# The two heads' first scores in one slot: shifting dense products by two scores in a fused attention and MLP kernel

## The chip, the cores and the metric

The kernel runs on one core of one Trainium2 chip. The metric is the device time of one execution in microseconds (us). The kernel before takes 1265.47 us (median of 3 runs, 1265.09 to 1265.52).

## The reference

One input of 2048 tokens by 512 channels goes through two branches that are mixed by a gate for each token:

```python
H = 32; Dh = D // H                                   # S = 2048, D = 512, F = 1792
q, k, v = (x @ wqkv) split into 32 heads of 16
p = softmax((q @ k^T) * Dh**-0.5)                     # 32 x 2048 x 2048
a = (p @ v, heads joined) @ wo
h = layernorm(x)
u = gelu(einsum("bsd,sf->bdf", h, w1) + b1)           # over tokens
b = einsum("bdf,fs->bds", u, w2) + b2, transposed
g = sigmoid((x * gate_w).sum(-1))
out = g * a + (1 - g) * b
```

All of it is in float32. Where the kernel uses single-pass float32 products, it splits an operand in a high and a low part and adds three products.

## The kernel before, in words

**Stages.** Up to about 278 us the kernel makes v, k, half of q and the first layer of the MLP. All that follows but the last few microseconds is one long loop of 128 *phases* (line 994), and the change is in this loop. Dense work that is left (the second MLP layer, the other half of q, the first half of the output projection) is done inside the loop, beside the attention scores.

**A phase.** Two heads and half of the queries (1024) make a *group*; 32 groups of four phases each. A phase makes 16 *scores*: score n is one product of 128 keys by 512 queries of one head, transposed (keys on partitions), 64 rows deep (16 channels in three split products and a shift). Head 0's operands lie on partitions 0 to 63 and head 1's on 64 to 127, so a score uses half of TensorE's rows. The other half can at the same time do a *dense product* (line 1076), half of the rows of a 128-row product; the other 64 rows are done in the next phase. Even phases (`second` = 0) have their scores on head 0 and dense halves on rows 64 to 127, odd phases (`second` = 1) the other way round. Two matmuls that run side by side are called a *slot* here. A phase has `n_b` = 14 dense products (96 phases) or 12 (32 phases): in phases 0 to 63, the last two of every eight have 12 (a late query block), phases 64 to 111 all have 14, and phases 112 to 127 all have 12 (the output projection). A score that has no dense product beside it is paired with a score of the other head, which `head` says. A group's first phase is called ph 0.

**What becomes of a score.** It lies in PSUM, in one of seven banks, and goes one of three ways:

```python
EVAC = 1, 3, 5, 9, 14, 15        # VectorE copies it to SBUF (L1089); one long exp over all six (L1102)
SINGLE = 0, 2, 4, 6, 7, 8        # ScalarE's exp reads it from PSUM (L1093)
TWO = (10, 11), (12, 13)         # ScalarE's exp reads two neighbouring banks at once (L1031)
TURNS = [(0, 2), (4, 6), (7, 8), *TWO]
HELD = [(1, 3), (5, 9), (14, 15)]
```

ScalarE (ACT) does in each phase six single exps in order of n, two double ones, and the long exp; nothing else in most of the loop. The profile names the scores' tiles s (scores 0 to 9), t (10 to 13) and u (14 and 15).

**Banks.** Scores 0 to 6 take the seven banks. Score 7 takes that of score 0 (freed by the first single exp), 8 that of score 1 (first copy), 9 that of score 2 (second single). Scores 10 and 11 take those of 3 and 4 (second copy, third single), 12 and 13 those of 5 and 6 (third copy, fourth single), 14 that of 7 (fifth single), 15 that of 9 (fourth copy). The result of p @ v, `av`, takes that of score 8 (sixth single).

**The end of a phase.** `apply_v` (line 953) multiplies the exps with v in 64 matmuls of 128 rows by 32 columns, four side by side: first the pairs HELD of the phase before, then the pairs TURNS of this one. VectorE (DVE) then adds `av` to the group's sums (L985). In ph 0 the held pairs are the last of the group before and go to a bank of their own, so there are adds for `av` and adds for a second bank (`t`). Which part of the bank an add covers follows from the heads of the pairs: if all pairs have one head, one add of 128x256; two adds, 128x256 and 64x256, if one pair has both heads; one add of 128x512 if all is met.

**Order.** The loop is under `manual_schedule`, so every engine executes in the order in which the program is written. The copies of the next phase stand behind the adds of this one in DVE's queue. A token that GpSimd (POOL) writes after a phase's last dense product (L1080) keeps the first dense product of the next phase behind it, since both add to the same bank `dn`. When the last product of a dense block is done, DVE reads `dn`: at the end of the phase in most cases, but in the eight second phases of a late query block a copy `begin` (L616) is put ahead of the copies of scores 14 and 15 (line 1084), at the score before the last.

Of the kernel before, what the change touches and what calls it, by code (L numbers as in the profile page):

```python
# [60 lines left out]
def gated_mix(ctx: ExitStack, tc: tile.TileContext, a_x, a_wqkv, a_wo, b_w1, b_b1, b_w2, b_b2, gate_w, out):  # L61
# [55 lines left out]
    def bank():  # L117
        return acc.tile([P, NB], F32, name="acc")
# [59 lines left out]
    with tc.tile_pool(name="vp", bufs=1, side="right") as pool:  # L178
# [122 lines left out]
        for t in range(2, NS):  # L301
# [9 lines left out]
            ps = bank()  # L311
# [51 lines left out]
    if True:  # L363

        def project(w, n):
            ps = bank()
            cols = slice(n * NB, (n + 1) * NB)
            hi, lo = w
            products(ps, [((hi[:, k, :], lo[:, k, :]), (xt_hi[:, k, cols], xt_lo[:, k, cols])) for k in range(ND)])
            return ps  # L370
# [12 lines left out]
        for b in range(ND):  # L383
            wk_b, wq_b = qk_w.pop(0), qk_w.pop(0)
            kmax = bd.tile([P, NQ], F32, name="kmax")
            for at, (n, keys) in enumerate(jobs):
                ps = project(wk_b if keys else wq_b, n)
# [38 lines left out]
    with tc.tile_pool(name="gl", bufs=2, side="right") as gl:  # L426
# [22 lines left out]
        beside = {mybir.EngineType.Activation, mybir.EngineType.DVE, mybir.EngineType.Pool}  # L449
# [51 lines left out]
        for f0, cs in order.items():  # L501
            n = min(NB, F - f0) // P
            ps = [bank() for _ in range(n)]
# [77 lines left out]
    PHASES, NSC, BANKS = 4, 16, 7  # L581
# [295 lines left out]
    for t in range(NS):  # L877
        at = put(second_layer(t), at, [14] * 3)
        if queries:
            b, n = queries.pop(0)  # L880
# [53 lines left out]
    def regions():  # L934
        return tc.tile_pool(name="ps_s", bufs=1, space=PSUM, reuse_waits="tile")
# [3 lines left out]
    def column_halves(x):  # L939
        x = x.rearrange("p (i m c) -> p m i c", i=2, m=2)  # L940
        return x[:, 0], x[:, 1]
# [48 lines left out]
    with tc.manual_schedule(engines=engines):  # L990
        held, fence, turn, spare = [], None, 0, 0
        landed.clear()

        for p in range(LAST + 1):
            grp, ph = divmod(p, PHASES)
            second = ph % 2
# [10 lines left out]
            if not second:  # L1007
                beside = [step(*args) for step, *args in dense.get(p // 2, ())]
            n_b = len(beside)
            half = slice(0, HALF) if second else slice(HALF, P)  # L1010

            head = [second if n < n_b else (second + NSC - 1 - n) % 2 for n in range(NSC)]
            if n_b == NSC - 2:
                head[-2:] = second, 1 - second
            else:
                head[-4:] = second, 1 - second, 1 - second, second
            in_turn = list(range(n_b)) + ([14, 15] if n_b == NSC - 2 else [12, 13, 15, 14])
            qbs = {}
            for a, b in TURNS + HELD:
                if head[a] == head[b]:  # L1020
# [6 lines left out]
            def exps(n):  # L1027
                pt = ptp.tile([P, 2, NB], F32, name="p2", bufs=len(TWO))
                where = [share[(j - BANKS) % BANKS] for j in (n - 1, n)]
                low = min(where)  # L1030
                pairs_done.append(nc.scalar.activation(pt, twos[low, low + 1], AF.Exp, scale=SCALE))  # L1031
                for j, k in zip((n - 1, n), where):
                    units[j] = *units[j][:3], pt[:, k - low, :]
# [8 lines left out]
            for n in in_turn:  # L1042
                i, qb = head[n], qbs[n]
                c = at[i][qb]
                at[i][qb] += 1
                if n < TWO[0][0]:
                    if n >= BANKS:
                        ones[share[n - BANKS]] = psum.tile([P, NB], F32, name=f"s{share[n - BANKS]}")
                    s = ones[share[n % BANKS]]
                else:  # L1050
                    if n == TWO[0][0]:
                        pool.__exit__(None, None, None)
                        pool = regions()
                        psum = pool.__enter__()
                        twos = {}
                        for low in range(BANKS):
                            if low == share[1]:
                                av = psum.tile([P, NB], F32, name="av")
                            elif low in (share[0], share[2]):
                                twos[low] = psum.tile([P, NB], F32, name=f"u{low}")  # L1060
                            elif low not in twos:
                                two = psum.tile([P, 2, NB], F32, name=f"t{low}")
                                twos[low], twos[low + 1] = two[:, 0, :], two[:, 1, :]
                                twos[low, low + 1] = two
                    s = twos[share[2 if n == NSC - 1 else (n - BANKS) % BANKS]]
                rows_i = slice(i * HALF, i * HALF + ROWS)
                nc.tensor.matmul(  # L1067
                    s,
                    kt[grp][rows_i, c * P : (c + 1) * P],
                    qt[grp][rows_i, qb * NB : (qb + 1) * NB],  # L1070
                    start=True,
                    stop=True,
                )
                if n < n_b:
                    ps, a, b, begin, last, done = beside[n]
                    mm = nc.tensor.matmul(ps, a[half], b[half], start=begin and not second, stop=last and bool(second))  # L1076
                    if n == 0 and fence is not None:
                        tc.add_manual_dep(mm.ins, fence.ins.name, SYNC, reason=REASON)
                    if n == n_b - 1:
                        fence = nc.gpsimd.memset(token, 0.0)  # L1080
                        tc.add_manual_dep(fence.ins, mm.ins.name, SYNC, reason=REASON)
                if n == in_turn[-2]:
                    if n_b and second and beside[-1][-1] in between:
                        between[beside[-1][-1]]()
                    for what, *args in amid.get(p, ()):
                        what(*args)
                if n in EVAC:
                    pt = evac[:, EVAC.index(n), :]
                    nc.vector.tensor_copy(pt, s)  # L1089
                    units[n] = i, c, qb, pt  # L1090
                elif n in SINGLE:
                    pt = ptp.tile([P, NB], F32, name="p1", bufs=len(SINGLE))
                    one = nc.scalar.activation(pt, s, AF.Exp, scale=SCALE)  # L1093
                    if n == SINGLE[-1] and p:
                        tc.add_manual_dep(one.ins, earlier.ins.name, SYNC, reason=EARLY)
                    units[n] = i, c, qb, pt
                else:
                    units[n] = i, c, qb, None
                    if n in (TWO[0][1], TWO[1][1]):
                        exps(n)  # L1100
            for x in ([evac] if p < LAST else [evac[:, :2, :], evac[:, 2:, :]]):
                done = nc.scalar.activation(x, x, AF.Exp, scale=SCALE)  # L1102
# [45 lines left out]
    with (  # L1148
# [17 lines left out]
        last = column_halves(last_ot)  # L1166
# [63 lines left out]
    with tc.If(far_off != 0):  # L1230
        with (
# [6 lines left out]
            for b in range(ND):  # L1238
                with tc.For_i(0, P // DH, 1) as hi:
# [11 lines left out]
                    for t in range(NS):  # L1251
# [4 lines left out]
                        m = pool.tile([P, 1], F32, name="m")  # L1256
# [54 lines left out]
```

## Time and profile before

| | |
|---|---|
| median of the runs | 1265.47 us (1265.09 to 1265.52) |
| profiled execution | 1265.31 us, of which the span of its instructions 1263.5 us |
| granted TensorE clock | 0.999 |
| loop of phases | first single exp at 278.1 us, the last exp ends at 1229.5 us (1226.48 + 2.97) |

How to read the rows: a group of instructions is given with its line, engine, operation, out<-in tiles and shape, its count, the engine's busy time, the mean duration in ns, and the idle time before it with what ended it. In a timeline a row has start, duration (of the whole run of like instructions that are merged to one row, xcount), engine, line and operation, and in brackets the idle time before it. PE are matmuls, PEld their weight loads. Durations of neighbouring instructions of one engine overlap, so the step from start to start is shorter than the duration. Matmul ends are modelled.

### The profile page before, as it was taken

The numbers are of one execution on the slowest core, as the hardware profiler recorded it, in microseconds if no ns is written. First come the engines' busy times: TensorE is split into PE (matmuls) and PEld (weight loads), VectorE is DVE, ScalarE is ACT, GpSimd is POOL, SyncE is SP. The second block draws the span as 40 slices with busy tenths as digits, with TensorE's granted clock in tenths as the row PEclk, the third lists the DMA queues.
The fourth block names the chain that finished last, engine by engine and source line by source line (L and its number), as shares of the span: only waits on it lengthen the run. The fifth ranks groups of instructions, "written<-read, shape, count | busy, mean of one in ns | idle before, by whom it ended". The sixth has DMA issues, their size and how long they took to land.

```text
span 1263.5 us, 32833 instructions
## 1 busy us (share of the span) xinstructions
PE 1254.8 (99%) x13342; PEld 829.2 (66%) x13342; DVE 856.7 (68%) x1562; ACT 1069.0 (85%) x1405; POOL 198.6 (16%) x316
## 2 busy tenths in 40 slices
PE   9999999999999999999999999999999999999998
PEld 7888888875666666666666666666666666666656
DVE  5675453178767676767677677776777677678883
ACT  4443343269999999999999999999999999999990
POOL 0220444461010101010110101111111111000000
PEclk9999999999999999999999999999999999999999
DMA  4799443244744444544344433444543443366611
GB/s 134 251 340 329 143 122 106 81 127 110 214 121 104 90 102 85 158 86 97 77 105 94 99 90 83 91 87 81 113 101 73 90 100 60 56 166 175 151 60 70
DMA packets 100556, 152.32 MB, mean 121 GB/s; under 512 B 17109, under 2 KB 56171, under 8 KB 96300
## 3 DMA queue, kind: packets, MB, share of 16 engines
q1 hardware_dynamic: 99820, 149.08, 46.0%
q8 instruction: 107, 1.75, 0.6%
q10 hardware_dynamic: 576, 1.05, 0.2%
q14 instruction: 53, 0.43, 0.1%
HBM read 105.39 MB, written 44.68 MB: 119 GB/s over the span
## 4 chain that ended last, share of the span: by engine, by line
PE 96%; DVE 2%; ACT 1%; issue 0%; DVEq 0%
PE av L963 31%; PE s L1067 21%; PE acc L424 12%; PE t L1067 9%; PE acc L75 8%; PE t L963 5%; PE dn L1076 3%; PE u L1067 3%; PE pa L1162 2%; DVE pe L1089 1%; PE acc L199 1%; PE acc L268 0%; DVE ot L985 0%; PE acc L245 0%; ACT p L1093 0%; ACT pe L1102 0%
## 5 line engine op out<-in xcount | busy, mean ns | idle before, releaser
L1093 ACT ACTIVATE p<-s 128x512 f32<-128x512 f32 x768 | 411.9, 789 | 0.1
L1102 ACT ACTIVATE pe<-pe 128x3072 f32<-128x3072 f32 x129 | 380.9, 2954 | 0.0
L1067 PE MATMUL s<-qs,ks 64*128 64x512 f32 x1280 | 329.8, 400 | 0.6 <-ACT p L1093 0.6
L1089 DVE COPY pe<-s 128x512 f32<-128x512 f32 x512 | 323.6, 685 | 5.5 <-PE s L1067 1.5
L1067 PEld LDWEIGHTS s<-qs,ks 64*128 64x128 f32 x1280 | 225.7, 184 | 92.7 <-issue 52.3
L1031 ACT ACTIVATE p<-t 128x1024 f32<-128x1024 f32 x256 | 278.7, 1267 | 0.0
L963 PE MATMUL av<-p,v 128*32 128x256 f32 x3880 | 227.2, 379 | 0.0
L1089 DVE COPY pe<-u 128x512 f32<-128x512 f32 x256 | 164.8, 685 | 67.1 <-PE u L1067 67.1
L963 PE MATMUL av<-pe,v 128*32 128x256 f32 x3072 | 192.5, 383 | 0.0
L985 DVE TENSOR_TENSOR ot<-av,ot 128x512 f32<-128x512 f32 (+2 forms) x160 | 93.0, 582 | 140.9 <-PE av L963 139.6
L68 POOL TENSOR_TENSOR w_lo<-w_raw,w_hi 128x512 fp32r<-128x512 f32 (+1 forms) x128 | 153.0, 1202 | 196.8 <-ACT w_hi L67 99.9
L1076 PE MATMUL dn<-u_lo,w_hi 64*128 64x512 f32 x448 | 181.0, 404 | 0.0
L1076 PE MATMUL dn<-u_hi,w_hi 64*128 64x512 f32 x448 | 180.7, 403 | 0.0
L963 PEld LDWEIGHTS av<-p,v 128*32 128x32 f32 x3880 | 126.0, 110 | 83.3 <-ACT p L1093 0.2
L1076 PE MATMUL dn<-u_hi,w_lo 64*128 64x512 f32 x448 | 180.6, 403 | 0.0
L1067 PE MATMUL t<-qs,ks 64*128 64x512 f32 x512 | 142.5, 413 | 0.0
L963 PEld LDWEIGHTS av<-pe,v 128*32 128x32 f32 x3072 | 86.8, 109 | 80.7 <-ACT p L1093 35.7
L1080 POOL MEMSET token<- 1x1 f32 x128 | 11.3, 88 | 742.7 <-PE dn L1076 679.4
L67 ACT CAST w_hi<-w_raw 128x512 fp32r<-128x512 f32 (+1 forms) x67 | 38.0, 569 | 82.7 <-PE acc L424 63.1
L1067 PEld LDWEIGHTS t<-qs,ks 64*128 64x128 f32 x512 | 73.2, 184 | 50.8 <-ACT p L1093 48.6
L424 PE MATMUL acc<-h_hi,w_hi 128*128 128x512 f32 x224 | 87.9, 392 | 0.0
L424 PE MATMUL acc<-h_hi,w_lo 128*128 128x512 f32 x224 | 87.9, 392 | 0.0
(171 smaller groups left out, 1615.8 us busy)
## 6 DMA issues: line engine op xcount, KB each, us to landing
w_raw<-in_B_w_dram SPq DMA_DIRECT2D x96, 256.0 KB
ks<-kp SPq DMA_DIRECT2D x192, 128.0 KB
qs<-qp SPq DMA_DIRECT2D x256, 64.0 KB
kp<-pc SPq DMA_DIRECT2D x16, 512.0 KB
qp<-pc SPq DMA_DIRECT2D x8, 768.0 KB
qp<-row SPq DMA_DIRECT2D x24, 256.0 KB
v<-v SPq DMA_DIRECT2D x4, 1088.0 KB
x<-in_A_x_dram SPq DMA_DIRECT2D x16, 256.0 KB
```

Source lines behind the costliest of these rows:

```text
L67: copy(hi, src)
L68: return sub(lo, src, hi.bitcast(F32), ALU.subtract)
L75: nc.tensor.matmul(ps, a, b, start=start and n == 0, stop=stop and n == last)
L424: nc.tensor.matmul(p, a, b, start=first and k == 0, stop=last and k == 2)
L963: mm = nc.tensor.matmul(av[32 * j : 32 * (j + 1), i * QC : (i + 1) * QC], vb[b][:, v_at : v_at + 32], pt[:, h * QC : (h + 1) * QC], start= ...
L985: latest["add"] = nc.vector.tensor_tensor(x, y, x, ALU.add)
L1031: pairs_done.append(nc.scalar.activation(pt, twos[low, low + 1], AF.Exp, scale=SCALE))
L1067: nc.tensor.matmul(s, kt[grp][rows_i, c * P : (c + 1) * P], qt[grp][rows_i, qb * NB : (qb + 1) * NB], start=True, stop=True,)
L1076: mm = nc.tensor.matmul(ps, a[half], b[half], start=begin and not second, stop=last and bool(second))
L1089: nc.vector.tensor_copy(pt, s)
L1093: one = nc.scalar.activation(pt, s, AF.Exp, scale=SCALE)
L1102: done = nc.scalar.activation(x, x, AF.Exp, scale=SCALE)
```

## The change

The order in which a phase's scores are paired is changed. Before, score n stood beside dense product n from the first slot on, and the scores that were left over stood at the end: 14 and 15 as a pair of the two heads (`n_b` = 14), or 12 and 13 and then 15 and 14 (`n_b` = 12). After, scores 0 and 1 are a pair of the two heads in the first slot, dense product m stands beside score m + 2, and where there are 12 dense products scores 14 and 15 are a second pair of the two heads at the end. The scores are issued in plain order.

With it, other scores belong to the other head: score 1, and with 12 dense products score 15 too, where it was score 15 (14 dense products) or 13 and 14 (12). So with 12 dense products all pairs in TURNS now have one head; the pair (1, 3) in HELD has both.

```diff
-            head = [second if n < n_b else (second + NSC - 1 - n) % 2 for n in range(NSC)]
-            if n_b == NSC - 2:
-                head[-2:] = second, 1 - second
-            else:
-                head[-4:] = second, 1 - second, 1 - second, second
-            in_turn = list(range(n_b)) + ([14, 15] if n_b == NSC - 2 else [12, 13, 15, 14])
+            head = [second] * NSC
+            head[1] = 1 - second
+            if n_b < NSC - 2:
+                head[-1] = 1 - second
+            in_turn = range(NSC)
...
-                if n < n_b:
-                    ps, a, b, begin, last, done = beside[n]
+                m = n - 2
+                if 0 <= m < n_b:
+                    ps, a, b, begin, last, done = beside[m]
                     mm = nc.tensor.matmul(ps, a[half], b[half], start=begin and not second, stop=last and bool(second))
-                    if n == 0 and fence is not None:
+                    if m == 0 and fence is not None:
                         tc.add_manual_dep(mm.ins, fence.ins.name, SYNC, reason=REASON)
-                    if n == n_b - 1:
+                    if m == n_b - 1:
                         fence = nc.gpsimd.memset(token, 0.0)
                         tc.add_manual_dep(fence.ins, mm.ins.name, SYNC, reason=REASON)
```

## The prediction

> **What bounds the kernel now.** I read the page's busy line and costliest groups first, then the timeline of ScalarE (ACT), then that of PE and VectorE (DVE) in one phase.
>
> ```profile
> PE 1254.8 (99%) x13342; PEld 829.2 (66%) x13342; DVE 856.7 (68%) x1562; ACT 1069.0 (85%) x1405; POOL 198.6 (16%) x316
> ...
> L1093 ACT ACTIVATE p<-s 128x512 f32<-128x512 f32 x768 | 411.9, 789 | 0.1
> L1102 ACT ACTIVATE pe<-pe 128x3072 f32<-128x3072 f32 x129 | 380.9, 2954 | 0.0
> ...
> L1089 DVE COPY pe<-s 128x512 f32<-128x512 f32 x512 | 323.6, 685 | 5.5 <-PE s L1067 1.5
> ```
>
> PE looks full, but a matmul's end is modelled. The exps are what counts: no idle time stands before them (0.1 and 0.0 us).
>
> ```profile
> 709.36 3.24 ACT L1093 ACTIVATE p<-s 128x512 f32<-128x512 f32 x6
> 712.23 2.19 ACT L1031 ACTIVATE p<-t 128x1024 f32<-128x1024 f32 x2
> 714.08 3.00 ACT L1102 ACTIVATE pe<-pe 128x3072 f32<-128x3072 f32 x1
> 716.77 3.24 ACT L1093 ACTIVATE p<-s 128x512 f32<-128x512 f32 x6
> ```
>
> One phase on ACT: six single exps, two double ones, one exp over the six copied scores; 716.77 - 709.36 = 7.41 us, and 128 phases of it are most of the span. Is ACT the limit, or is it fed at just that pace? A disturbed stretch tells:
>
> ```profile
> 857.72 3.25 ACT L1093 ACTIVATE p<-s 128x512 f32<-128x512 f32 x6
> 860.60 2.21 ACT L1031 ACTIVATE p<-t 128x1024 f32<-128x1024 f32 x2
> 862.73 2.77 ACT L1102 ACTIVATE pe<-pe 128x3072 f32<-128x3072 f32 x1
> 865.40 3.02 ACT L1093 ACTIVATE p<-s 128x512 f32<-128x512 f32 x6
> ...
> 872.73 3.12 ACT L1093 ACTIVATE p<-s 128x512 f32<-128x512 f32 x6
> ...
> 880.05 3.21 ACT L1093 ACTIVATE p<-s 128x512 f32<-128x512 f32 x6
> ```
>
> Here the long exp began 862.73 - 860.60 = 2.13 us after the double ones, against 714.08 - 712.23 = 1.85: 0.28 late. Afterwards the six singles start every 7.33 and 7.32 us, but they end at 868.42, 875.85 and 883.26: every 7.43 and 7.41. So ends come at 7.41 to 7.43 a phase whatever the starts do. Of the 0.28 lost at 862.73, only 880.05 - 857.72 - 3 x 7.41 = 0.10 was left three phases later. I read this as ACT's own pace, 7.42, with a lead: in the quiet phase instructions are begun about 3.24 - 3.02 = 0.22 us before their turn. That lead is the cover under which PE or DVE may be late at no cost.
>
> Now who feeds it:
>
> ```profile
> 708.82 0.50 PE L1067 MATMUL s<-qs,ks 64*128 64x512 f32 x1
> ...
> 712.01 0.39 PE L1067 MATMUL t<-qs,ks 64*128 64x512 f32 x1
> 712.01 0.38 PE L1076 MATMUL dn<-u_hi,w_hi 64*128 64x512 f32 x1
> 712.24 0.43 PE L1067 MATMUL u<-qs,ks 64*128 64x512 f32 x2
> 712.65 1.50 PE L963 MATMUL av<-pe,v 128*32 128x256 f32 x24
> 713.97 2.34 PE L963 MATMUL av<-p,v 128*32 128x256 f32 x40
> 716.24 0.50 PE L1067 MATMUL s<-qs,ks 64*128 64x512 f32 x1
> ```
>
> A loop is seen: score 0 at 708.82, its exp 0.53 later (716.24 to 716.77), the sixth single ends at 709.36 + 3.24 = 712.60, which frees the bank of av; av starts at 712.65, and the next score 0 follows 716.24 - 712.65 = 3.59 later. 0.53 + 3.24 + 0.05 + 3.59 = 7.41: closed. With ACT without its lead (3.02) it would be 7.19, so the PE side has 0.22 to spare, and no more.
>
> **The change part by part.** The instructions are the same in number and shape: 16 scores, 14 (96 phases) or 12 (32 phases) dense products, 9 exps, 6 copies, 64 av matmuls a phase, and the DMAs and their order stay. A slot, two matmuls side by side, costs 712.24 - 712.01 = 0.23, and there are 15 or 14 before and after. What moves:
>
> (1) *Start of a phase.* Score 1 takes the place of the first dense product in the cold slot; scores 2 to 14 come one slot earlier. Nothing is gained by it: exps go in ACT's order, and the banks of scores 7 to 13 come free at the pace of exps and copies. Zero for the slot itself. The first dense product waits for POOL's token of the phase before, which now comes one slot later, but some 3.5 us of av hide that. SP and POOL are passed by nothing else.
>
> (2) *End of a phase with 14.* Today scores 14 and 15 share a slot at 712.24; now each stands beside a dense product, one slot more behind the second pair of scores. Two rows tell when av may start:
>
> ```profile
> 1120.50 0.50 PE L1067 MATMUL u<-qs,ks 64*128 64x512 f32 x2
> 1120.93 0.42 PE L963 MATMUL av<-pe,v 128*32 128x256 f32 x3
> ```
>
> Here av starts 0.07 before the modelled end of the scores (1121.00), and so does the next score 0 after av (713.97 + 2.34 = 716.31, start 716.24). A slot of 0.39 (712.01) thus holds av back 0.32 from its start, not 0.23. The Trainium skill's page "TensorEngine Tiling (Array Packing)", Key Properties, says that changing the tiling mode drains TensorE; both rows agree, and it speaks against this change, since the slot before the switch is never overlapped. Without a drain the sum below would be 0.09 less and the loop hidden.
>
> When can score 12, the first of the last four, start? It needs the bank that the copy of score 5 frees:
>
> ```profile
> 708.96 0.69 DVE L985 TENSOR_TENSOR ot<-av,ot 128x512 f32<-128x512 f32 x1 [1.85 <-PE av L963]
> 709.59 2.52 DVE L1089 COPY pe<-s 128x512 f32<-128x512 f32 x4
> ```
> ```profile
> 710.79 0.68 DVE L1089 COPY pe<-s 128x512 f32<-128x512 f32 x1
> ```
> ```profile
> 1117.07 0.87 DVE L985 TENSOR_TENSOR ot<-t,ot 128x256 f32<-128x256 f32 x2 [1.33 <-issue]
> 1117.96 2.48 DVE L1089 COPY pe<-s 128x512 f32<-128x512 f32 x4
> ```
> ```profile
> 1119.37 0.18 PEld L1067 LDWEIGHTS t<-qs,ks 64*128 64x128 f32 x1 [0.29 <-ACT p L1093]
> ```
> ```profile
> 1119.71 0.39 PE L1067 MATMUL t<-qs,ks 64*128 64x512 f32 x1
> ```
>
> The copies queue behind the add of av, which waits for the end of av; so an earlier score doesn't hurry them. The copy of score 5 ends at 710.79 + 0.68 = 711.47, 2.65 after score 0. The weight load behind a copy: in the DVE-bound phase the second copy ends at 1117.96 + 0.60 + 0.68 = 1119.24 (0.60 from (2.48 - 0.68) / 3) and the load starts 0.13 later. The row blames ACT, so the price is bounded: 0.05 (av behind the sixth single) to 0.13; I take 0.12, as this load has the same two waits. From load to the second matmul is 1119.71 - 1119.37 = 0.34. The loop through DVE is then 2.65 + 0.12 + 0.34 (score 13) + 0.23 (14) + 0.23 (15) + 0.32 (drain) + 3.59 = 7.48, and with 0.05 it is 7.41. By ACT's waits alone (the fifth single frees the bank of score 14; without lead it ends 0.53 + 4 x 0.48 + 0.62 = 3.07 after score 0, 0.48 being a sixth of 712.23 - 709.36 and 0.62 what is left of 3.02; then 0.05, 0.34 to score 15, 0.32 and 3.59) it is 7.37. So 7.48 against 7.42: 0.06 a phase.
>
> Not in all phases: behind the first phase of a group the add is short.
>
> ```profile
> 701.60 0.42 DVE L985 TENSOR_TENSOR ot<-t,ot 128x256 f32<-128x256 f32 x1 [1.04 <-issue]
> 702.17 1.29 DVE L1089 COPY pe<-s 128x512 f32<-128x512 f32 x2 [0.15 <-PE dn L1076]
> ```
>
> There the copies waited 0.15 for score 1, which is now in the first slot: the DVE loop is 0.15 shorter, 7.33, and ACT's waits give 7.37; 0.05 of lead is won back. A group of four 14-phases costs 3 x 0.06 - 0.05 = 0.13. Phases 64 to 111 are twelve such groups: 1.6 us.
>
> (3) *End of a phase with 12.* Scores 12 and 13 take two slots, 14 and 15 share the last, as in a 14-phase today: 2.65 + 0.12 + 0.34 + 0.23 + 0.32 + 3.59 = 7.25. Free, and lead is won back. In phases 0 to 63 every eight hold four long loops (+0.24), two short ones (-0.10) and two of 12 (up to -0.17 each, as far as lead is missing): zero.
>
> (4) *The eight late-query phases* (L616). The DVE copy of dn stands ahead of the copies of scores 14 and 15:
>
> ```profile
> 333.70 0.68 DVE L616 CAST row<-dn 128x512 fp32r<-128x512 f32 x1
> 334.37 1.29 DVE L1089 COPY pe<-u 128x512 f32<-128x512 f32 x2
> ```
>
> Today it fits into DVE's pause, as its last dense product stands beside score 11. Now it stands beside score 13: 2.65 + 0.12 + 0.34 + 0.39 + 0.04 = 3.54 after score 0, ending at 4.21; the two copies then end at 5.50 and the long exp starts at 5.60 (0.10 behind, 714.08), against 714.08 - 708.82 = 5.26 today: 0.34 late. The disturbance of 0.28 above cost 0.10 with a full lead; here the lead is partly used up: 0.10 to 0.34. I take 0.28: 8 x 0.28 = 2.2 us.
>
> (5) *Adds.* In the last 16 phases the first phase of a group needs two adds (1117.07, 0.87) since scores 12 and 13 are of two heads; now one of 0.42. Its copies come up to 0.45 sooner, in four phases; most was caught up by the lead, so between 0 and 0.26 each; I take 0.1: -0.4 us.
>
> Sum: 1.6 + 2.2 - 0.4 = +3.4 us. The profiled execution took 1265.31 (span 1263.5 and 1.8 around it), 0.16 below the median of 1265.47; 1265.47 + 3.4 = 1268.9. With all bounds at once (0.05 or 0.13 behind a copy, 0.10 or 0.34 late, 0.26 or 0 for the adds) it is 0 + 0.8 - 1.0 = -0.2, or 12 x 0.16 + 8 x 0.04 + 2.7 = +4.9; each 0.01 that I misread in the loop is 0.7 more over the 72 long phases, so the forecast itself, the loop through DVE above ACT's pace, goes from +1.2 to about +6.
>
> **The rivals.** *A, all hidden.* If the load behind a copy needs 0.05, the loop is 7.41 and (2) costs nothing; (4) costs 8 x 0.12 at the full lead: +1.0 - 0.4 = +0.6, 1266.1. For it: the ACT rows show the lead at work. Against: the load at 1119.37.
>
> *B, the lead is no lead.* If the longer singles are only instructions that wait inside ACT for something else, their ends don't move forward and every slot at the end counts: scores 14 at 712.24, 15 at 712.47, av at 712.79 instead of 712.65, 0.14 x 96 = 13.4, and (4) at 0.34 x 8 = 2.7: +16, 1281.6. It decides if the singles still take 3.24 in a slowed phase; 865.40 (3.02) speaks against it.
>
> *C, faster.* If the copies were what sets the pace, having score 1 in the first slot would take away DVE's waits before them: at most the 5.5 us of the copies' row, and the 0.4 to 1.0 of (5); half of it would give 1262. It decides if av waits for a copy; at 712.65 it starts 0.05 behind ACT instead, so I hold it unlikely.
>
> **How the numbers follow.** 0.2% is 2.5 us, about what a measurement of this kernel can tell from no change. The forecast gets 0.62, A 0.18, B 0.14, C 0.06. Of the forecast's +1.2 to +6 I put 0.46 above +2.5. Slower: 0.46 + 0.14 = 0.60; within: 0.16 + 0.18 = 0.34; faster 0.06. The forecast and A hold 0.80, so the range is theirs with some of the way to B, where the lead counts in part: 1265.0 to 1277.0.
>
> **What would show it.** Right: in 14-phases from 64 to 111 a score 15 alone in the last slot, av 0.32 behind its start and 0.2 or more behind the end of the sixth single; six singles of about 3.05 instead of 3.24; phases of 7.48 three times in four. In late-query phases the copies of u start at about 4.2 and the long exp some 0.3 late. Wrong: singles still 3.24 with av 0.05 behind them (A), or 3.24 and phases of 7.55 (B), or phases below 7.40 (C).

## The result, and the profile after

The changed kernel takes 1268.93 us (median of 9 runs, 1268.64 to 1269.18) against 1265.50 for the kernel before (9 runs beside them): +3.43 us, ratio 1.0026, 95% interval 1.0017 to 1.0034. Forecast were 1268.9 and 1265.0 to 1277.0. The profiled execution has a span of 1266.8 us against 1263.5.

The page after the change, the same two exps as before the change and the copies:

```profile
PE 1259.2 (99%) x13342; PEld 823.1 (65%) x13342; DVE 843.7 (67%) x1547; ACT 1072.5 (85%) x1405; POOL 198.7 (16%) x316
...
L1093 ACT ACTIVATE p<-s 128x512 f32<-128x512 f32 x768 | 394.2, 650 | 0.1
L1102 ACT ACTIVATE pe<-pe 128x3072 f32<-128x3072 f32 x129 | 365.9, 2839 | 0.1
L1089 DVE COPY pe<-s 128x512 f32<-128x512 f32 x512 | 317.6, 681 | 1.0 <-PE s L1066 0.8
```

As many exps, and still no idle time before them that the profile counts. Yet a single exp takes 650 ns on average instead of 789: the kernel is slower and the instructions of the engine that set its pace before are *shorter*. That is the lead of the prediction being spent. The timeline of ACT in the quiet part, four phases in a row:

```profile
1025.04 3.04 ACT L1093 ACTIVATE p<-s 128x512 f32<-128x512 f32 x6
...
1032.53 3.05 ACT L1093 ACTIVATE p<-s 128x512 f32<-128x512 f32 x6
...
1039.92 3.07 ACT L1093 ACTIVATE p<-s 128x512 f32<-128x512 f32 x6
...
1047.40 3.04 ACT L1093 ACTIVATE p<-s 128x512 f32<-128x512 f32 x6
```

The steps are 7.49, 7.39 and 7.48 where they were 7.41 to 7.42, and the six singles take 3.04 to 3.07 instead of 3.24. What paces them is seen in the phase that starts at 1024.51, in the timelines of PE, DVE and the weight loads (one fence each):

```profile
1024.51 0.50 PE L1066 MATMUL s<-qs,ks 64*128 64x512 f32 x2
```
```profile
1024.64 0.69 DVE L985 TENSOR_TENSOR ot<-av,ot 128x512 f32<-128x512 f32 x1 [0.82 <-PE av L963]
1025.25 2.47 DVE L1089 COPY pe<-s 128x512 f32<-128x512 f32 x4
...
1026.45 0.68 DVE L1089 COPY pe<-s 128x512 f32<-128x512 f32 x1
```
```profile
1027.24 0.18 PEld L1066 LDWEIGHTS t<-qs,ks 64*128 64x128 f32 x1 [0.27 <-ACT p L1093]
```
```profile
1027.58 0.39 PE L1066 MATMUL t<-qs,ks 64*128 64x512 f32 x1
...
1027.81 0.39 PE L1066 MATMUL u<-qs,ks 64*128 64x512 f32 x1
...
1028.05 0.39 PE L1066 MATMUL u<-qs,ks 64*128 64x512 f32 x1
1028.08 0.39 PE L1076 MATMUL dn<-u_lo,w_hi 64*128 64x512 f32 x1
1028.40 1.50 PE L963 MATMUL av<-pe,v 128*32 128x256 f32 x24
...
1031.99 0.50 PE L1066 MATMUL s<-qs,ks 64*128 64x512 f32 x2
```

Read from the top: score 0 (with score 1 beside it) at 1024.51, the copy of score 5 ends at 1026.45 + 0.68 = 1027.13, the load of score 12 starts 0.11 later, score 13 at +0.34, 14 at +0.23, 15 at +0.24, av at +0.35, the next score 0 at +3.59: 7.48. The sixth single ended at 1025.04 + 3.04 = 1028.08; av starts 0.32 behind it, where it was 0.05. The load's row names ACT, but the load follows the copy: over the long loops of phases 64 to 111 it starts 0.116 behind the copy of score 5 (median) after the change and in `pair89` below alike, while its distance to the fourth single is 0.13 and 0.17. Where the copy comes early, behind a short add, it starts 0.051 behind the fourth single.

Where the 3.3 us of span went, from the first singles of phases 4, 64, 112 and 127, before and then after:

```profile
308.77 3.24 ACT L1093 ACTIVATE p<-s 128x512 f32<-128x512 f32 x6
753.85 3.25 ACT L1093 ACTIVATE p<-s 128x512 f32<-128x512 f32 x6
1109.98 3.25 ACT L1093 ACTIVATE p<-s 128x512 f32<-128x512 f32 x6
1221.81 3.08 ACT L1093 ACTIVATE p<-s 128x512 f32<-128x512 f32 x6
```
```profile
308.97 3.08 ACT L1093 ACTIVATE p<-s 128x512 f32<-128x512 f32 x6
756.56 3.01 ACT L1093 ACTIVATE p<-s 128x512 f32<-128x512 f32 x6
1114.58 3.04 ACT L1093 ACTIVATE p<-s 128x512 f32<-128x512 f32 x6
1225.68 3.24 ACT L1093 ACTIVATE p<-s 128x512 f32<-128x512 f32 x6
```

| stretch | before | after | difference |
|---|---|---|---|
| to phase 4 | 308.77 | 308.97 | +0.20 |
| phases 4 to 64 (late queries) | 445.08 | 447.59 | +2.51 |
| phases 64 to 112 (all 14) | 356.13 | 358.02 | +1.89 |
| phases 112 to 127 (all 12) | 111.83 | 111.10 | -0.73 |
| from there to the end | 41.69 | 41.12 | -0.57 |

A start can be early by the lead, and the lead is not the same at the ends of these stretches: the singles of the four rows take 3.24, 3.25, 3.25 and 3.08 before, and 3.08, 3.01, 3.04 and 3.24 after. By the ends of the sixth singles the differences are +0.04, +2.43, +1.92, -0.36 and -0.73. The ends are what ACT's pace is read from, so they are the better measure of what was lost.

The last row isn't the loop: DVE's last instruction stands 35.52 and 35.59 us after the same point; the rest is how long the last store took. From that instruction's end to the end of the span it is 5.46 before and 4.80 after, so the loop alone lost about 4.0 us. In the profiles of all runs (those below too) this rest is 4.6 to 5.1 in the five kernels with the new pairing in the late-query phases, and 5.5 to 5.7 in the six others (one profile each). What shortens it no run shows; a total can so be lower than the stretches of the loop add up to.

In the late-query phases, here one on DVE and then on ACT:

```profile
393.85 0.69 DVE L616 CAST row<-dn 128x512 fp32r<-128x512 f32 x1 [0.38 <-PE dn L1076]
394.46 1.28 DVE L1089 COPY pe<-u 128x512 f32<-128x512 f32 x2
```
```profile
390.84 3.13 ACT L1093 ACTIVATE p<-s 128x512 f32<-128x512 f32 x6
393.70 2.10 ACT L1030 ACTIVATE p<-t 128x1024 f32<-128x1024 f32 x2
395.83 2.77 ACT L1102 ACTIVATE pe<-pe 128x3072 f32<-128x3072 f32 x1
398.50 3.02 ACT L1093 ACTIVATE p<-s 128x512 f32<-128x512 f32 x6
```

The copy of dn now waits 0.38 for its product, the copies of scores 14 and 15 queue behind it, and the long exp starts 2.13 after the double ones (1.85 in the quiet phase before). The next singles start 7.66 later. But by their ends, 393.97 and 401.52, it is 7.55: 0.13 is lost, the rest was lead.

### The profile page after: what moved, and what is told of

Read it like the earlier page. It is cut to its first block, busy times and chain, and to the rows that moved or that the text cites. A ratio compares the mean times of both kernels' runs of the same rounds, so it can differ in the third digit from the quotient of the medians.

```text
span 1266.8 us, 32814 instructions
## 1 busy us (share of the span) xinstructions
PE 1259.2 (99%) x13342; PEld 823.1 (65%) x13342; DVE 843.7 (67%) x1547; ACT 1072.5 (85%) x1405; POOL 198.7 (16%) x316
## 4 chain that ended last, share of the span: by engine, by line
PE 97%; ACT 2%; DMA 0%; DVE 0%; issue 0%; SPq 0%; ACTq 0%; DVEq 0%
PE av L963 30%; PE s L1066 20%; PE acc L424 12%; PE t L1066 10%; PE acc L75 8%; PE t L963 5%; PE u L1066 4%; PE dn L1076 3%; PE pa L1162 2%; ACT pe L1102 1%; PE acc L199 1%; ACT p L1093 1%; PE acc L268 0%; DMA x<-in_A_x_dram 0%; ACT p L1030 0%; PE dn L1162 0%
## 5 line engine op out<-in xcount | busy, mean ns | idle before, releaser
L1093 ACT ACTIVATE p<-s 128x512 f32<-128x512 f32 x768 | 394.2, 650 | 0.1
L1102 ACT ACTIVATE pe<-pe 128x3072 f32<-128x3072 f32 x129 | 365.9, 2839 | 0.1
L1089 DVE COPY pe<-s 128x512 f32<-128x512 f32 x512 | 317.6, 681 | 1.0 <-PE s L1066 0.8
L1066 PE MATMUL s<-qs,ks 64*128 64x512 f32 x1280 | 301.8, 412 | 0.7 <-ACT p L1093 0.6
L1066 PEld LDWEIGHTS s<-qs,ks 64*128 64x128 f32 x1280 | 200.8, 184 | 96.0 <-issue 52.3
L1030 ACT ACTIVATE p<-t 128x1024 f32<-128x1024 f32 x256 | 260.4, 1124 | 0.0
L1066 PE MATMUL t<-qs,ks 64*128 64x512 f32 x512 | 160.1, 429 | 0.0
```

What stands on the lines that cost most here:

```text
L1066: nc.tensor.matmul(s, kt[grp][rows_i, c * P : (c + 1) * P], qt[grp][rows_i, qb * NB : (qb + 1) * NB], start=True, stop=True,)
```

## The experiments

The theory: ACT's own pace is 7.41 to 7.42 a phase; a lead of some 0.2 us covers what is late on PE or DVE; after the change the loop through the copy of score 5 is above that pace. The rivals: each phase pays for itself, with no lead; the late-query copy is the whole cost; score 15 alone before av costs by itself; the pair in the first slot of a phase costs ("cold" below: its matmuls take 0.50 by their row, the others 0.39). All times are medians beside runs of the kernel before on the same chip (1265.54 to 1265.69). The stretches are taken as in the table above, from each run's own profile, by starts where nothing else is said.

**One part at a time.** `new14` pairs in the new way where there are 14 dense products, `new12` where there are 12. Of the edit only the two lines that tell which scores are shifted are shown; the heads and the order follow `ahead`.

```diff
+            ahead = 2 if n_b == NSC - 2 else 0        # new12: if n_b < NSC - 2
...
-                m = n - 2
+                m = n - ahead
```

Expected of new14:

> The new pairing in the 96 phases with 14 dense products alone; the 32 with 12 are as before. Theory (DVE loop above ACT's pace, ACT's lead as a buffer between phases): phases 64 to 111 lose 1.9 us as after the change (long loops 7.48, short 7.39); in phases 0 to 63 the two 12-phases of every eight win the lead back and the late-query copy is in time, so 0 to 0.4 us there; phases 112 to 127 as before. Together +2.0 us, about 1267.5. Rival (each phase pays for itself, no buffer): 72 long loops at 0.06 = +4.5 us, 1270. Rival (the late-query copy is the whole cost): 1265.5.

Measured: 1269.11 us, ratio 1.0028 (1.0017 to 1.0038). Phases 64 to 112 lose 2.14, near the 1.9 expected; but phases 4 to 64 lose 1.25, not 0 to 0.4. The rows of ACT say why, at two 12-phases (383.49 and 390.91) and the 14-phase behind them (398.27):

```profile
383.49 3.07 ACT L1101 ACTIVATE p<-s 128x512 f32<-128x512 f32 x6
390.91 3.06 ACT L1101 ACTIVATE p<-s 128x512 f32<-128x512 f32 x6
398.27 3.12 ACT L1101 ACTIVATE p<-s 128x512 f32<-128x512 f32 x6
```

The ends are 386.56, 393.97 and 401.39, 7.41 and 7.42 apart: ACT's pace. The two phases with room give lead back, 0.05 here (3.07 to 3.12), and no time. What a long loop has lost beyond the lead stays lost. The copy in the late-query phases is not the whole cost, as it is in time here; neither does each phase pay in full (4.5).

> The new pairing in the 32 phases with 12 dense products alone; those with 14 are as before. Theory: the long exp of the eight late-query phases is 0.3 late, but the lead is full (0.2) when it comes, so about 0.1 each, 0.8 us; phases 112 to 127 win 0.7 us by the missing adds. Together +0.1 us, 1265.6, and with the kernel of the 14-phases alone the two halves do not add up to the whole of +3.4. Rival (costs add up, no buffer): 8 x 0.3 - 0.7 = +1.7 us, 1267.2.

Measured: 1265.16, ratio 0.9996 (0.9986 to 1.0005): no difference that can be told. The parts are there in the profile: phases 4 to 64 lose 1.19, by the ends 0.94 or 0.12 for each late exp, and phases 112 to 127 gain 0.50, by the ends 0.33. So the loop lost some 0.6 us; the total doesn't show it, as the rest behind DVE's last instruction is 0.85 shorter (4.61), and that it came out near the forecast of +0.1 is partly luck. One late-query phase, whose lead is full when it comes:

```profile
390.54 3.25 ACT L1101 ACTIVATE p<-s 128x512 f32<-128x512 f32 x6
...
398.30 3.02 ACT L1101 ACTIVATE p<-s 128x512 f32<-128x512 f32 x6
```

The start is 7.76 later, the end (393.79 to 401.32) 7.53. By the rival the eight would have cost 2.4.

**Where the pair stands.** In `pair1314` and `pair89` the 14-phases have their pair of two heads later in the phase; 12-phases as before. The lines that place the dense products are left out here.

```diff
-            head[1] = 1 - second
+            head[14] = 1 - second     # slots: 0 to 12 with dense products, 13 beside 14, 15 with a dense product
...
+            head[9] = 1 - second      # pair89: 0 to 7 with, 8 beside 9, 10 to 15 with
```

> In phases with 14 dense products scores 13 and 14 share a slot (score 14 of the other head), 12 stands beside a dense product before them and 15 alone with one behind them; the 12-phases as before. Score 15 is the last slot before av as after the change, but only two slots lie behind score 12 instead of three. Theory: loop through DVE 2.62 + 0.12 + 0.34 + 0.23 + 0.32 + 3.59 = 7.22, through ACT's fifth single 7.39: both under ACT's pace, so no cost: 1265.3 to 1265.9, with singles of 0.60 to 0.65 instead of 0.79 and av 0.2 behind the sixth single. Rival (score 15 alone in the last slot before the drain costs by itself): +0.14 x 96 at most and as much as in the kernel of the 14-phases alone at least, 1267.5 or more.

Measured: 1265.94, ratio 1.0003 (0.9994 to 1.0012). Phases 4 to 112 lose 0.06 together. In a phase of it, PE's last scores and ACT:

```profile
1023.81 0.67 PE L1070 MATMUL u<-qs,ks 64*128 64x512 f32 x2
1024.15 0.39 PE L1080 MATMUL dn<-u_lo,w_hi 64*128 64x512 f32 x1
1024.47 1.07 PE L963 MATMUL av<-pe,v 128*32 128x256 f32 x16
```
```profile
1021.17 3.08 ACT L1097 ACTIVATE p<-s 128x512 f32<-128x512 f32 x6
```

Score 15 has the last slot to itself before av, and av is 0.22 behind the sixth single (1024.25), which is shorter too. But one slot less lies behind score 12, the lead covers it, and nothing is lost. So a last slot of its own is not what costs.

> In phases with 14 dense products scores 8 and 9 share a slot (score 9 of the other head), 0 to 7 have dense products 0 to 7 beside them and 10 to 15 dense products 8 to 13; the 12-phases as before. Theory: what counts is that no pair lies behind score 12, so as in the kernel of the 14-phases alone, +2.0 us (1267.5); the short loops behind the first phase of a group are not short by score 1 here, so up to 0.5 us more. Rival (the pair of two heads in the cold first slot is what costs): 1265.5.

Measured: 1273.83, ratio 1.0065 (1.0051 to 1.0079): +8.1 us, far more than I had expected. Here every phase is long:

```profile
1020.60 3.05 ACT L1097 ACTIVATE p<-s 128x512 f32<-128x512 f32 x6
...
1028.12 3.05 ACT L1097 ACTIVATE p<-s 128x512 f32<-128x512 f32 x6
```
```profile
1035.30 0.42 DVE L985 TENSOR_TENSOR ot<-t,ot 128x256 f32<-128x256 f32 x1 [1.33 <-issue]
1035.87 1.29 DVE L1093 COPY pe<-s 128x512 f32<-128x512 f32 x2
```

7.52 in long and short ones alike. The copies start 0.77 after score 0 in both (median), since they wait for score 1, which is in the second slot again; after the change they start at 0.75, and at 0.57 behind a short add. The pair early costs as expected, and score 1 in the first slot, which the pair89 kernel lacks, is a *gain* inside the change: 0.03 in long loops and 0.12 in short ones. The rival of the first slot falls.

**The copies as the cause.** `short_add` lets DVE add half of av where it adds all of it, in the changed kernel; so half of these sums is left out.

```diff
-            parts = [(ot, av)]
+            parts = [(ot[:, :QC], av[:, :QC])]
```

> The changed kernel; where DVE adds all of av (128x512) it adds the left half (128x256) alone, so half of the sums is left out, and the copies of the next phase start some 0.17 sooner, as behind the first phase of a group. Theory (copy of score 5 sets the long loop): all 14-phases are short ones, 7.40 by the score loop, so ACT's 7.415 rules again: phases 64 to 111 cost 0 instead of 1.9 us, singles 0.6 with av 0.22 behind; in phases 0 to 63 the late exp remains, 8 x 0.2 = 1.6 instead of 2.5; the end as after. Together about 1265.9. Rival (score 15 alone in the last slot with the drain behind it, paced by ACT): the long loops stay at 7.48 and the time at 1268.9.

Measured: 1265.65, ratio 1.0001 (0.9992 to 1.0010). Phases 64 to 112 lose 0.06, phases 4 to 64 1.33, phases 112 to 127 gain 0.70.

```profile
1021.78 0.42 DVE L985 TENSOR_TENSOR ot<-av,ot 128x256 f32<-128x256 f32 x1 [0.81 <-PE av L963]
1022.21 2.48 DVE L1089 COPY pe<-s 128x512 f32<-128x512 f32 x4
```
```profile
1022.17 3.08 ACT L1093 ACTIVATE p<-s 128x512 f32<-128x512 f32 x6
...
1029.60 3.07 ACT L1093 ACTIVATE p<-s 128x512 f32<-128x512 f32 x6
```

With the add shorter by 0.27 the phase is 7.43 again, though score 15 still stands alone at the end. The long loop goes through DVE's add and copies: shown.

`begin_last` puts the copy L616 of the late-query phases behind the copies of scores 14 and 15.

```diff
-                    if n_b and second and beside[-1][-1] in between:
-                        between[beside[-1][-1]]()
...
             if n_b and second and beside[-1][-1]:
+                if beside[-1][-1] in between:
+                    between[beside[-1][-1]]()
                 beside[-1][-1]()
```

> The changed kernel with the copy of dn (L616) of the eight late-query phases behind the copies of scores 14 and 15 instead of ahead of them. Theory: the long exp is in time; phases 0 to 63 cost what they do in the kernel with the 14-phases alone or a little less, 0.9 to 1.25 us instead of 2.5, so about 1267.4. By the prediction's own sum (8 x 0.28 = 2.2 us for this copy, nothing for the rest up to phase 63) it would be 1266.7. Rival (the late copy is hidden by the lead): 1268.9.

Measured: 1267.98, ratio 1.0018 (1.0009 to 1.0027): phases 4 to 64 lose 1.23 instead of 2.51, by the ends 1.39 instead of 2.43. On DVE the copies are in time again:

```profile
394.03 1.29 DVE L1087 COPY pe<-u 128x512 f32<-128x512 f32 x2 [0.61 <-PE u L1066]
395.23 0.68 DVE L616 CAST row<-dn 128x512 fp32r<-128x512 f32 x1
```

So by the ends the late copy costs some 1.0 in eight phases, 0.13 each (1.28 and 0.16 by the starts; the medians of the two kernels' losses are 0.99 apart), and the rest of these phases 1.39. Why the two 12-phases of every eight don't make up for the long loops is seen in the singles of phases 15, 16 and 17, the first with 12 dense products, the others with 14:

```profile
390.78 3.15 ACT L1091 ACTIVATE p<-s 128x512 f32<-128x512 f32 x6
...
398.10 3.24 ACT L1091 ACTIVATE p<-s 128x512 f32<-128x512 f32 x6
...
405.69 3.07 ACT L1091 ACTIVATE p<-s 128x512 f32<-128x512 f32 x6
```

The lead is back in full at 3.24 and gone a phase later, as in each of these blocks, with ends 7.41 and 7.42 apart: no time is won. (In phase 16 the work moved behind holds the copies up by 0.10 too, so this phase alone doesn't settle it.) `short_add` shows how much lead a 14-phase can hold after the change: with the copies out of the way its singles stay at 3.07 to 3.08. There the load of score 14 starts 0.05 behind the end of the fifth single, which comes 3.11 after score 0; score 15 follows 0.34 later, av 0.33 and the next score 0 3.59 later, and that loop through ACT closes at 7.42. So it holds some 0.05 of lead, where it held 0.22 before, and what is won back beyond that helps one phase at most.

**A small price added.** One memset of 128x64 ahead of the copies, in the kernel before and in the changed one.

```diff
+            nc.vector.memset(tick, 0.0)
             for n in in_turn:
```

> The kernel before with one more DVE instruction in each phase, a memset of 128x64, ahead of the copies; about 0.1 us each, 13 us of DVE work in all. Theory: the loop through DVE is 7.33 to 7.42 with it, under or at ACT's pace: 0 to +0.8 us, 1265.5 to 1266.3, with shorter singles. Rival (no lead: what comes later is paid): +0.1 x 128 = +12 us.

> The changed kernel with the same memset ahead of the copies. Theory: the 72 long loops pay it in full, about 0.1 each, the 24 short ones what goes over ACT's pace, 0.06; the 12-phases little: +7 to +9 us over the changed kernel, 1276 to 1278. Rival (the long loop is set by ACT's singles and the slots at the end, not by the copies): no change, 1268.9.

Measured: 1266.60 for tick_before, ratio 1.0007 (0.9998 to 1.0016), and 1269.67 for tick_after, ratio 1.0032 (1.0020 to 1.0044), so 4.1 over the kernel before against 3.4 without the memset. My price was wrong, so this pair tells less than it should: the intervals of the two changed kernels overlap, and in tick_before the singles of phases 64 to 111 stay at 3.24 where shorter ones were expected. In tick_after:

```profile
711.80 0.11 DVE L1042 MEMSET tick<- 128x64 f32 x1
711.83 2.42 DVE L1091 COPY pe<-s 128x512 f32<-128x512 f32 x4
```

The copies start 0.07 later but four of them take 2.42 instead of 2.47, and the third ends only 0.02 later (medians 2.637 and 2.620 after score 0). The long loops grow by as much, from 7.483 to 7.500, which agrees with the theory in sign and size but is small. In tick_before phases 4 to 112 take 801.2 us as before; what it loses, 0.71, is in phases 112 to 127, where the two adds already hold the copies up.

**A version of both.** `proj` pairs in the new way in phases 112 to 127 alone.

> The new pairing in phases 112 to 127 alone; all others as before. Theory: there the two adds become one, no phase of 7.66 is left and the lead is kept: -0.7 us, nothing lost elsewhere: 1264.8, the best of all. Rival (the new pairing always costs at a phase's end or start): not faster than before, 1265.5 or more.

Measured: 1265.12 against 1265.64, ratio 0.9998 (0.9989 to 1.0007). The profile has the gain in the expected place, 0.54 in phases 112 to 127 (0.36 by the ends) and nothing in phases 4 to 112, but the runs cannot tell it from no change. No version clearly beats the kernel before.

## Why the prediction was right, and where its sum was not

The forecast of +3.4 was met by +3.43, but two of its terms were off in opposite senses, and the loop alone lost about 4.0.

- *What bounds the kernel.* Right: ACT's ends come at 7.41 to 7.42 a phase wherever it is fed, and the longer singles are lead. Rival B is refuted by the singles of 0.6 us in slowed phases and by new12; rival A by the loop of 7.48; rival C by the direction.
- *Step (1), the start.* "Nothing is gained by it" was a little wrong: the copies start 0.02 sooner (0.745 instead of 0.766 after score 0, medians), and pair89 shows 0.03 a long loop.
- *Step (2), the end of a 14-phase.* Right in mechanism and size: 7.48 forecast, medians of 7.483 (long) and 7.395 (short, forecast 7.37). Two parts were off by 0.03 and cancel: the copy of score 5 ends at 2.62 instead of 2.65, and the wait before av is 0.35 instead of 0.32, because the dense half beside score 15 runs 0.03 behind it (1028.05 and 1028.08) and av waits for that one (1028.08 + 0.39 - 0.07 = 1028.40). Twelve groups cost 1.9 for 1.6. With the 0.23 of a slot in place of the 0.35 the long loop would be 7.36, an estimate by this sum, under ACT's pace. The rule of the Trainium skill's page "TensorEngine Tiling (Array Packing)", Key Properties, that a change of tiling mode drains TensorE, agrees with this 0.35, but no run here takes the change of tiling away. The 72 long loops that the range was worked out with are 68 by the prediction's own count (36 in phases 64 to 111 and four in each of the eight blocks ahead); the sum of 3.4 doesn't use that number.
- *Step (3), phases 0 to 63 even.* Wrong, the term that failed: forecast 0, measured 1.23 (begin_last) or 1.25 (new14), by the ends 1.39 and 1.28. I had set the short loops and the 12-phases against the long ones as time. They give back lead only, as ACT's ends never come closer than 7.41 (phases 4 to 127 of all eleven profiles). The 12-phases did win back the 0.17 that I had put down for them (3.07 to 3.24 in begin_last), but a 14-phase holds only some 0.05 of lead after the change (3.07 in short_add), so of the four long loops in eight phases only the first is covered: their ends come at 7.42, 7.46, 7.49 and 7.49 in begin_last (medians).
- *Step (4), the late-query copy.* Right in mechanism (the copies of u start 4.2 after score 0, the long exp is about 0.3 late), too large in size: 0.28 each forecast, 0.13 measured by the ends, so 1.0 us instead of 2.2. It was within the bounds given, 0.10 to 0.34. The singles ahead of the late exp are still 3.13 long, so more of the lead was there than I took; as new12 loses 0.12 with the full lead, how the loss depends on the lead stays open.
- *Step (5), the adds.* Right: -0.36 for -0.4 by the ends (-0.73 by the starts, as phase 127 had lost part of its lead before the change); phases 112 to 127 run at ACT's pace with a full lead:

```profile
1144.05 3.24 ACT L1093 ACTIVATE p<-s 128x512 f32<-128x512 f32 x6
...
1151.47 3.25 ACT L1093 ACTIVATE p<-s 128x512 f32<-128x512 f32 x6
```

Steps (3) and (4) together were forecast at 2.2 and measured at 2.43, from two terms that were both off. With the 0.3 more of step (2) the loop lost about 0.6 more than the sum, and the last store, which the sum doesn't have, took 0.66 less in the profile. That the sum fits to 0.03 is luck; what the runs bear out is the loop through DVE.

## What to carry to other kernels

An engine that shows no idle time can be the pace setter or be fed at just that pace; the duration of its instructions tells. If they are longer than behind a disturbance, there is a lead, and changes elsewhere cost nothing until it is spent; from there on they cost in full, and later phases with room restore the lead, not the time. How much lead a phase can hold depends on its own loop through that engine: here 0.22 before the change and 0.05 after it. Before moving work within a loop, sum up every closed loop through it (here ACT, PE with ACT, and PE with DVE) against the slowest one, for each kind of phase by itself, and look at what stands ahead in an in-order queue, as the add ahead of the copies does here.

## What the runs showed of the hardware

A DVE memset of 128x64 took 0.112 us by its own row. In tick_after the copies behind it start 0.07 later, but the end of the third moves by only 0.02, as the copies are shorter.

The same weight load starts 0.116 behind a DVE copy when the copy comes last (after, pair89, pair1314, tick_after; medians), and 0.051 behind an ACT exp when that does (short loops of after, short_add).

Of two matmuls side by side, av waits for the one that ends later: with starts 0.03 apart it stands at 1028.40, 0.07 before the modelled end of the later, and in pair1314 too, with the dense half at 1024.15 and av at 1024.47.
